# Attention's out products on the two row halves of TensorE, two token tiles together

## The chip, the cores and the metric

The kernel runs on one core of a Trainium2 chip. The metric is the device time of one execution in microseconds (us). Of the kernel before there are three runs, with a median of 717.38 us (716.96 to 717.64).

## What is computed

Eight sequences of 576 tokens pass through three stages. The change touches the first of them, a linear attention of 8 heads with 64 channels each:

```python
kv  = einsum('bhsd,bhse->bhde', k, v)        # one 64 x 64 matrix for a head
out = einsum('bhsd,bhde->bhse', q, kv)       # the out product
out = out / sqrt(mean(out**2, -1) + 1e-6) * g_norm
x   = out.transpose(0, 2, 1, 3).reshape(B, S, 512)
gate = sigmoid(causal conv of 5 taps over x, for each channel)
x = (gate * (x @ w_val)) @ w_out             # stage 2
h = gelu(x @ w_in); u, v = halves of h       # stage 3
x = x + (u * (w_sg @ layernorm(v) + b_sg)) @ w_out2
```

All of it is in float32. Stages 2 and 3 split each operand of a matmul into a high and a low part; the kv and out products are plain fp32 matmuls.

## The kernel before

Attention and stage 2 run together for a batch after the other, with several batches in flight; stage 3 follows for all batches. The tokens of a batch are four tiles of 128 and a fifth (number 4) that reaches back, TOK = [0, 128, 256, 384, 448], of which the last 64 columns are used. The 512 channels are four blocks j of 128, two heads each.

For a batch, `kv` (line 364) multiplies keys and values head by head into the two column halves of TensorE (line 379: 40 matmuls, with outputs on partitions 0 to 63 and 64 to 127). `kv_out` (line 384) copies the results into a block diagonal, `kvbd` (64 x 64 blocks, zeros beside them). `product` (line 395) makes the out product of one token tile: for each block j the q block (128 channels x 128 tokens) is the operand that is loaded, and `kvbd` (128 x 128) is the one that streams; the four results fill one PSUM bank of 512 words, all channels of 128 tokens. Then follow for the tile: `square` on ScalarE, `sums` on VectorE, `mean` and `root` on GpSimd, `scale` on VectorE (or ScalarE), `turn` (four transposes on TensorE into another bank), and from there `high` and `full` on ScalarE and `low` on VectorE, which write 4 channel blocks x 128 tokens of the operands of stage 2 and of the convolution (`taps`, `tap`). Channel block m of the convolution needs the tokens of all five tiles.

The order of all instructions is written out by hand in two strings, ORDER and STEADY, that a loop (line 950) walks through. In them o31 is batch 3's out product of tile 1; q, r, m, w, s, t are square, sums, mean, root, scale and turn; h, x and l are high, full and low; p is a tap, S a sigmoid; v and y are the two matmuls of stage 2 with z, Z, u and Y behind them; a, b and D are the splits of the weights (a1l is a matmul among them); kv3a and kv3b are the halves of kv. A number behind ~ puts that many small filler matmuls ahead of an operation (line 322). L stands for loads, all on SP's queue: LK1 loads k and v of batch 1, La1 a quarter of w_val (512 KB), LK0a and LV0a 512 KB of k and v, LM3 clears a part of V on GpSimd (`clear`, line 337). For batches 0 to 2 that clear was part of LK or LV (lines 356, 866, 875). Each engine works through its own instructions in this order. PSUM has eight banks, which `bank` (line 140) hands out in turn.

Of the kernel before, what the change touches and what calls it, by code (L numbers as in the profile page):

```python
# [44 lines left out]
r11 b0h p023 p001 o13 a2c r12 p002 m12 b11 p024 p030 m11* w11 o10 q14 q13 b12 b0l r13 q10 Lb3 r10 w12 Lb2 p031 v01 b0c
m13* S02 Lq2 p003 b13 p010 m10 w13 s11* w10 v03 s13* p032 s10* p011 t11 kv2 LK3 LM3 v00 p004 p012 p033 b1h v02 S00 k2a
p013 s12* b14 b20 p014 S01 b1s p034 z01 r14 z00 k2b h11 b2a S03 t13 Z01 b1+ Z00 g0L m14* t10 b21 t12 x13 x11 w14 b30
h10 s14 o22 o21~3 u00* l11 g0r z03 h13 Z03 z02 l10 l13 t14 h12 o24 l12 o23 b22 u01* o20 Lq3 LDa LDb q24 x10 q23 b3a
r23 Z02 q22 u03* x14 q20 q21 x12 b31 m23* w23 b23 b32 r22 b24 r21 r20 u02* m20* p110 b33 p120 r24 v11 p111 v12 p121
# [8 lines left out]
Z20 w31 p232 p233 s30 u20* o33 Dat LM4 s31 t30 q33 v22 Db0 h30 r33 q32 z21 m33* S22 w33 p234 Dba Y11 r32 g2X o34 Db1
S23 m32* s33 w32 Z21 t31 z22 v23 Y10 u21 g2r x31 g2L LDc Db2 q34 Lq4 Db3 Z22 x30 u22* kv4a/0-8 z23 Dbh h31 kv4a/8-12
s32 Z23 r34 kv4b Db4 m34* Dbs LDd t32 w34 u23 LK5 y20/0-11 h32 Dbt x32 Dca Dc1 Dc0 Dc2 t33 s34 y21/0-5 h33 l32 k4 l33  # L60
y20/11-1 y21/5-7 x33 Dc3 Dc4 Dch l31 LDe Dcs t34 y22 Dct x34 l30 p300 Dda p301 p310 p302 p320 o40 Y21 p303 y23 p330
p311 g3X Y20 Dd0 p312 q40 p304 o41 p321 S30 r40 v30 q41 p331 m40* w40 p322 Dd1 Dd2 p313 o42 r41 v31 q42 s40 m41* w41
Y22 z30 p323 p314 o43 p324 S31 Z30 t40 p332 v32 q43 r42 Y23 p333 S32 m42* u30* s41 r43 o44 z31 w42 z32 Z31 t41 Lq5 v33
p334 q44 m43* Z32 w43 Dd3 s42 Ddh S33 u31 g3r u32* s43 t42 r44 y30/0-9 Dds z33 m44* Dd4 Z33 LM5 Ddt LDf w44 h42 u33
t43 x42 y31/0-9 De0 Dea x40 s44 h41 g3L l42 x41 y30/9-2 x43 De1 y31/9-2 De2 y30/11-1 De3 y31/11-1 Deh t44 De4 y32 Des
LDg x44 Det p430 Df0 l41 p420 p410 y33 Dfa p411 p400 p431 Y32 Y31 p401 p412 v80 Y33 Df1 h40 Df2 p402 v81 p413 p421
kv5a/0-8 l40 kv5a/8-12 p403 kv5b p404 z80 v82 k5 z81 Y30 Df3 v83 Z81 z82 Z80 LK6 u81 Z82 u80* o50 z83 Dfh p414 o51 q50
Dfs h43 r50 y80/0-5 g4X u82* y81/0-5 l43 q51 y82/0-1 Z83 y80/5-1 r51 y81/5-1 y82/1-5 m50* Df4 w50 y83/0-4 Dft LDh
y80/6-2 p422 y81/6-2 Dga y82/6-2 y83/4-1 y80/8-1 Dg0 y81/8-1 m51* y82/8-1 u83 y83/5-2 w51 y80/9-2 y81/9-2 p432 y82/9-2
y83/7-4 Dg1 v40/0-3 Dg2 Dg3 Dgh y80/11-1 s50 y81/11-1 y82/11-1 y83/11-1 Dgs Y81 v40/3-9 S40 Dg4 s51 Y82 LDi Y83 p433  # L70
S41 o52 p423 t50 Dgt q52 t51 p424 Dha v41 Y80 p434 Dh0 Dh1 Dh2 Dh3 Dhh z40 Dhs o53 Z40 LM6 Dh4 v42 z41 LDj q53 r52 S43
Dht Z41 m52* g4L u40* Dia x51 h51 o54 Di1 w52 Di0 Di2 v43 r53 q54 Lq6 Dih Di3 S42 u41 Dis m53* Di4 w53 z42 LDk
kv6a/0-8 Dit Z42 kv6a/8-12 r54 Dja s52 h50 kv6b m54* u42* z43 x50 s53 t52 Z43 LK7 w54 Dj0 g4r Dj1 h52 Dj2 Dj3 Djh u43
y40 x52 LM7 Djs l50 s54 t53 Dj4 y41 x53 l52 LDl h53 Djt Dk0 Dka k6 Dk1 Dk2 Y40 Dk3 t54 l51 Dkh y42 x54 Dks l53 p500
Dk4 Dkt p520 LDm p501 p530 p502 o60 Dla Dl1 p531 y43 q60 p510 p532 p503 p521 o61 Dl0 r60 v50 p522 q61 m60* w60 g5X Dl2
p511 p504 p512 o62 p523 v51 q62 r61 S50 s60 m61* Y43 w61 p533 Y41 p524 o63 r62 t60 p513 q63 m62* v52 Dlh s61 S52 Dl3
Y42 p514 Dls z50 S51 r63 Z50 o64 Dl4 m63* w62 Dlt t61 Lq7 z51 v53 h61 LDn p534 Dma w63 q64 Dm0 g5L Z51 z52 x61 u51 S53
# [1041 lines left out]
```

## Time and profile before

| | |
|---|---|
| time, median of three runs | 717.38 us |
| the profiled execution, its own time | 717.08 us |
| its span, first to last instruction | 715.3 us |
| TensorE multiplies / weight loads | 706.0 / 618.3 us |
| VectorE | 571.8 us |
| ScalarE / GpSimd | 362.2 / 163.4 us |

Engines are named as in the profile: PE is TensorE's multiplies, PEld its weight loads, DVE VectorE, ACT ScalarE, POOL GpSimd, SP the queue that issues transfers. A row of a timeline has the start and the length of a group of instructions in us, engine, line, operation, tile written and tiles read, rows and columns of TensorE in use, the shape, and the number of instructions. An fp32 matmul shows as two loads and two multiplies. The end of a multiply is modelled in the profile and reaches past the start of the next one, so the pace of matmuls is read from starts.

### The profile page before, as it was taken

What the parts mean: (1) busy time and instruction counts of PE and PEld (TensorE: products, weight loads), DVE (VectorE), ACT (ScalarE), POOL (GpSimd) and SP (SyncE); (2) the same over time, 40 slices, a digit from 0 to 9 for tenths busy, and PEclk for the clock granted to TensorE, in tenths of its full rate; (3) what the DMA queues carried; (4) which work ended last, traced back from release to release, by engine and by line L of the source; (5) the groups of instructions that cost most, each with busy time, mean ns of one, the idle gap of its engine ahead of it and who ended that gap; (6) DMA issues with size and microseconds to landing.
All of it is one profiled execution on the core that took longest, in us unless ns stands there. A gap on an engine that the chain in (4) does not pass through costs nothing.

```text
span 715.3 us, 11743 instructions
## 1 busy us (share of the span) xinstructions
PE 706.0 (99%) x4462; PEld 618.3 (86%) x4462; DVE 571.8 (80%) x1111; ACT 362.2 (51%) x747; POOL 163.4 (23%) x180
## 2 busy tenths in 40 slices
PE   7999999999999999999999999999999999999998
PEld 7788888889888888899889888898899898898897
DVE  3999898989999999799867877767857767868662
ACT  2999947574657574664424434325434334335220
POOL 1558435444636443121000000100100100100000
PEclk9999999999999999999999999999999999999999
DMA  9994046336534105541231222123241122111302
GB/s 306 323 298 164 31 170 239 115 111 229 197 100 155 75 31 169 164 149 32 81 112 30 75 89 59 53 66 89 77 144 43 62 74 75 59 60 45 103 1 89
DMA packets 57241, 81.20 MB, mean 114 GB/s; under 512 B 3680, under 2 KB 30304, under 8 KB 56160
## 3 DMA queue, kind: packets, MB, share of 16 engines
q1 hardware_dynamic: 57184, 80.45, 33.7%
q8 instruction: 35, 0.57, 0.3%
q14 instruction: 22, 0.18, 0.1%
HBM read 61.56 MB, written 18.87 MB: 112 GB/s over the span
## 4 chain that ended last, share of the span: by engine, by line
PE 59%; DVE 2%; DMA 1%; issue 0%; ACT 0%; SPq 0%; DVEq 0%; ACTq 0%
PE sg L740 17%; PE out L303 14%; PE hv L631 13%; PE hu L303 12%; PE hur L303 2%; DVE G L499 1%; DMA raw<-y_main 1%; PE y L303 1%; PE val L303 0%; DVE T L531 0%; ACT X1h L608 0%; DVE cv L196 0%; DVE cv L191 0%; DVE cv L187 0%; DVE X1l L609 0%
## 5 line engine op out<-in xcount | busy, mean ns | idle before, releaser
L499 DVE SCALAR_TENSOR_TENSOR G<-X,cw,G 128x576 f32<-128x576 f32 x128 | 101.8, 827 | 4.2 <-ACT G L496 3.9
L643 POOL TENSOR_TENSOR bmv<-bmv,mhalf 128x1 f32<-128x1 f32 x36 | 21.5, 596 | 342.4 <-DVE bmv L642 342.4
L303 PE MATMUL y<-Z,WOh 128*128 128x512 f32 (+1 forms) x320 | 96.2, 375 | 0.0
L631 PE MATMUL hv<-wiv,X1h 128*128 128x512 f32 x256 | 83.3, 390 | 0.9 <-ACT X1h L608 0.9
L303 PE MATMUL out<-Z,K 128*128 128x512 f32 x256 | 83.0, 389 | 0.0
L303 PE MATMUL hu<-X1h,wiu 128*128 128x512 f32 x256 | 79.2, 391 | 0.0
L421 POOL TENSOR_TENSOR st<-st,mhalf 128x8 f32<-128x8 f32 x40 | 73.1, 1839 | 2.2
L303 PEld LDWEIGHTS y<-Z,WOh 128*128 128x128 f32 x320 | 57.9, 188 | 9.7
L620 ACT ACTIVATE T<-T 128x512 f32<-128x512 f32 x68 | 42.9, 631 | 42.3 <-DVE T L617 42.2
L303 PE MATMUL y<-Z,WOl 128*128 128x512 f32 (+1 forms) x160 | 58.0, 368 | 0.0
L631 PEld LDWEIGHTS hv<-wiv,X1h 128*128 128x128 f32 x256 | 47.7, 188 | 10.8 <-ACT X1h L608 1.4
L303 PEld LDWEIGHTS out<-Z,K 128*128 128x128 f32 x256 | 48.1, 188 | 9.9
L741 DVE SCALAR_TENSOR_TENSOR T<-sg,gln,WOl 128x288 f32<-128x288 f32 x64 | 32.8, 516 | 26.3 <-PE sg L740 26.2
L303 PEld LDWEIGHTS hu<-X1h,wiu 128*128 128x128 f32 x256 | 46.6, 188 | 8.3
L303 PE MATMUL hu<-X1l,wiu 128*128 128x512 f32 x128 | 50.0, 390 | 0.0
L631 PE MATMUL hv<-wiv,X1l 128*128 128x512 f32 x128 | 49.9, 390 | 0.0
L303 PE MATMUL out<-Z,V 128*128 128x512 f32 x128 | 49.8, 389 | 0.0
L752 ACT ACTIVATE Z<-T 128x512 fp32r<-128x512 f32 x32 | 20.1, 631 | 58.2 <-DVE T L751 58.2
L400 PEld LDWEIGHTS o<-kvbd,Q 128*128 128x128 f32 x320 | 39.9, 191 | 2.6 <-ACT kvbd L391 0.5
L400 PE MATMUL o<-kvbd,Q 128*128 128x128 f32 x320 | 40.7, 275 | 0.3 <-ACT kvbd L391 0.3
L303 PE MATMUL val<-X0h,WV 128*128 128x512 f32 x128 | 40.7, 399 | 0.0
L303 PE MATMUL val<-X1h,WV 128*128 128x512 f32 x128 | 40.0, 396 | 0.0
(183 smaller groups left out, 1708.6 us busy)
## 6 DMA issues: line engine op xcount, KB each, us to landing
y_main<-Y SPq DMA_DIRECT2D x8, 1024.0 KB, 4.7
raw<-y_main SPq DMA_DIRECT2D x32, 256.0 KB, 3.1
Y<-y_main SPq DMA_DIRECT2D x32, 256.0 KB, 3.9
out_dram<-Y SPq DMA_DIRECT2D x32, 256.0 KB, 2.3
Q<-in_qT_dram SPq DMA_DIRECT2D x7, 1152.0 KB, 6.3
K<-in_k_dram SPq DMA_DIRECT2D x7, 1024.0 KB, 7.3
V<-in_v_dram SPq DMA_DIRECT2D x7, 1024.0 KB, 9.1
raw<-in_w_in_dram SPq DMA_DIRECT2D x16, 256.0 KB, 4.8
```

The source lines that it names most:

```text
L303: nc.tensor.matmul(ps, lhsT=a[:, kt, msl], rhs=x[:, kt], start=(i == 0), stop=(i == 3 * NK - 1))
L400: nc.tensor.matmul(po[:, j * P:(j + 1) * P], lhsT=self.q[:, j, o:o + P], rhs=bd[:, j, :], start=True, stop=True)
L421: nc.gpsimd.tensor_tensor(st[:, 2], st[:, 1], mhalf, op=ALU.pow)
L499: stt(gate[:, m], x32[:, m, j:j + S], cw3[:, m, j:j + 1], gate[:, m], op0=ALU.mult, op1=ALU.add)
L620: act(w, w, AF.Tanh, scale=CG * AG)
L631: nc.tensor.matmul(ps, lhsT=a[:, kt], rhs=p2["wiv"][:, w, kt], start=(i == 0), stop=(i == 3 * NK - 1))
L643: nc.gpsimd.tensor_tensor(mv[:, 3:4], mv[:, 2:3], mhalf[:, 0:1], op=ALU.pow)
L740: nc.tensor.matmul(ps, lhsT=a[:, msl], rhs=w, start=(n == 0), stop=(n == len(mm) - 1))
L741: later(0, lambda: stt(vs[:, sl], ps, gln_s[:, m:m + 1], p2["bsg"][:, sl], op0=ALU.mult, op1=ALU.add))
L752: act(g[:, 0], x, AF.Copy)
```

## The change

The out products of two token tiles are made together. For tiles 0 and 1 (and 2 and 3) there are two banks; for each tile, block j and half a, one matmul loads the q of one head (64 partitions x 128 tokens), on the row half a of TensorE, and streams the head's 64 x 64 block of kv, 64 columns, into bank a. A bank then holds four heads of 256 tokens in place of eight heads of 128. The fifth tile is made as before, four matmuls of 128 columns, written in two strips. On the host the heads of q, k and v are put in the order 0, 4, 1, 5, 2, 6, 3, 7, so that block j holds heads j and j + 4, and bank a the heads of a consecutive half. `turn`, `high`, `full` and `low` keep their four transposes and their 512 elements for each bank, now two channel blocks x 256 tokens (`part`). In the order's text o00 and o02 are then the pairs of batch 0, while q, r, m, w, s, t, h, x and l with number 0 to 3 stand for a bank each. The two order strings become one, newly written: it holds the same operations but for o with tiles 1 and 3, which are gone, and LM0, LM1 and LM2, which are now named. At the start K0a and K0b are loaded ahead of the quarters 1 and 0 of w_val.

```diff
@@ -37,54 +37,50 @@
 ORDER = """
-W30 La0 La1 LK0a LV0a LK0b LV0b LK0c LV0c Lq0a Lq0b Lg La2 La3 Lb0 Lcw a1a a0a a01 a00 a10 kv0a a02 a11 a12 kv0b a13
-a14 a03 k03b k01b a0h k02b k03a k02a k00b k01a k00a a04 o01~3 q01 o03 r01 a20 q03 LK1 o02 a2a r03 a21 q02 o04 a3a m01*
...
-"""
-
-STEADY = """
...
+LK0a LK0b La1 LV0a La0 W30 LV0b LV0c LK0c LM0 Lq0a La2 Lq0b Lcw Lg La3 a1a Lb0 a11 a10 kv0a a00 a0a a01 a02 a12 kv0b
+a13 a03 k01b k03a LK1 k01a k02a k02b k00a a0h k00b a04 a1h k03b o00~3 a14 a20 a2a a1l q01 a21 q00 a22 r01 a2h o02 c0
+a23 m01* w01 q02 o04 q03 a30 r02 q04 Lq1 r00 m02* ca Lb2 w02 a24 b0a a2l Lb1 a3a r03 LDa s01* c1 b00 m03* a31 w03 a32
...
+Dc0 g2r Z21 t32 z20 v22 Dc1 Z20 Dc2 g2L S22 u20* Dch h33 h32 Dc3 y21/0-5 l30 Dcs x33 l31 x32 t34 Dc4 z22 o42 LDe l32
+Z22 o40 u21 x34 q42 u22* l33 o44 q43 r42 q41 y20/0-11 Dct q40 m42* u23 w42 p330 Dd0 r41 Y11 p320 p331 m41* LM5 y23 q44
...
 """
@@ -393,11 +389,24 @@
                             nc.vector.tensor_copy(bd[h, j, h], pk[h, :, h])
 
         def product(self, t):
-            o, bd = TOK[t], kvbd[self.b % 2]
-            self.tile[t] = {"po": own(bank("o"))}
-            po = self.tile[t]["po"]
-            for j in range(NK):
-                nc.tensor.matmul(po[:, j * P:(j + 1) * P], lhsT=self.q[:, j, o:o + P], rhs=bd[:, j, :], start=True, stop=True)
+            bd = kvbd[self.b % 2]
+            if t == 4:
+                po = own(bank("o"))
+                self.tile[t] = {"po": po}
+                po = po.rearrange("p (a j e) -> p j a e", a=2, j=NK)
+                for j in range(NK):
+                    nc.tensor.matmul(po[:, j], lhsT=self.q[:, j, TOK[4]:], rhs=bd[:, j].rearrange("p (a e) -> p a e", a=2),
+                                     start=True, stop=True)
+                return
+            po = [own(bank("o")) for a in range(2)]
+            for a in range(2):
+                self.tile[t + a] = {"po": po[a]}
+            for i in range(2):
+                o = TOK[t + i]
+                for j in range(NK):
+                    for a in range(2):
+                        h, c = slice(a * DH, (a + 1) * DH), (i * NK + j) * DH
+                        nc.tensor.matmul(po[a][:, c:c + DH], lhsT=self.q[h, j, o:o + P], rhs=bd[h, j, h], start=True, stop=True)
 
         def square(self, t):
             i = self.tile[t]
@@ -430,24 +439,31 @@
                i["st"][:, 2].unsqueeze(2).to_broadcast([P, 8, DH]), op=ALU.mult)
 
         def turn(self, t):
-            i, n = self.tile[t], P if t < 4 else REST
+            i = self.tile[t]
             pt = own(bank("xT"))
+            if t == 4:
+                i["pt"] = pt.rearrange("p (j e) -> p j e", j=NK)[:, :, P - REST:]
+            else:
+                i["pt"] = pt.rearrange("p (m e) -> p m e", m=2)
             for j in range(NK):
-                nc.tensor.transpose(pt[:, j * P:(j + 1) * P], i["xo"][:, j * P:(j + 1) * P], ident)
-            i["pt"] = pt.rearrange("p (j e) -> p j e", j=NK)[:, :, P - n:]
+                c = j if t == 4 else j % 2 * 2 + j // 2
+                nc.tensor.transpose(pt[:, c * P:(c + 1) * P], i["xo"][:, j * P:(j + 1) * P], ident)
+
+        def part(self, x, t, o=0):
+            c = t // 2 * 2 * P + o
+            return x[:, t % 2 * 2:t % 2 * 2 + 2, c:c + 2 * P]
 
         def at(self, t):
-            o, n = (TOK[t], P) if t < 4 else (MAIN, REST)
-            return x32[:, :, HALO + o:HALO + o + n]
+            return self.part(x32, t, HALO) if t < 4 else x32[:, :, HALO + MAIN:]
 
         def high(self, t):
-            act(self.xh[:, :, TOK[t]:TOK[t] + P], self.tile[t]["pt"], AF.Identity, scale=gcol_s)
+            act(self.part(self.xh, t), self.tile[t]["pt"], AF.Identity, scale=gcol_s)
 
         def full(self, t):
             act(self.at(t), self.tile[t]["pt"], AF.Identity, scale=gcol_s)
 
         def low(self, t, by=None):
-            xh, xl = (x[:, :, TOK[t]:TOK[t] + P] for x in (self.xh, self.xl))
+            xh, xl = (self.part(x, t) for x in (self.xh, self.xl))
             if by is None:
                 stt(xl, self.tile[t]["pt"], gcol_s, f32(xh), op0=ALU.mult, op1=ALU.subtract)
             else:
@@ -863,7 +879,7 @@
             piece[0]()
             piece[2]()
         elif what in ("K0c", "V0c"):
-            atts[0].load_kv((), (kind == "V",))
+            atts[0].load_kv((), (kind == "V",), clear=False)
         elif kind in "KV" and i[0] == "0":
             atts[0].load_kv(K0[i[1]], (kind == "V",), False)
         elif kind == "M":
@@ -872,7 +888,7 @@
             w_piece(i)[0]()
         elif kind in "KV":
             if kind == "K":
-                atts[int(i)].load_kv(clear=int(i) < 3)
+                atts[int(i)].load_kv(clear=False)
         elif kind == "q":
             atts[int(i[0])].load_q({"a": ((0, 2 * P),), "b": ((2 * P, S),), "": ((0, S),)}[i[1:]])
         elif what == "cw":
@@ -957,11 +973,6 @@
                 busy(int(op[1:]))
             elif op in ("kv0a", "kv0b"):
                 atts[0].kv("ab".index(op[3]), False)
-            else:
-                act_part(op.rstrip("*"), op[-1] == "*")
-        for op in STEADY.split():
-            if op[0] == "L":
-                load(op[1:])
             else:
                 act_part(op.rstrip("*"), op[-1] == "*")
     marks = [latest()] * 4
@@ -1086,10 +1097,12 @@
     import concourse.bacc as bacc
     from concourse.bass_utils import run_bass_kernel_spmd as run
 
+    turn = [i + j for j in range(4) for i in (0, 4)]
+    q, k, v = (np.asarray(x)[:, turn] for x in (q, k, v))
     host = {
-        "qT": np.asarray(q).transpose(0, 1, 3, 2).reshape(B, NK, P, S),
-        "k": np.asarray(k).transpose(0, 2, 1, 3).reshape(B, S, D),
-        "v": np.asarray(v).transpose(0, 2, 1, 3).reshape(B, S, D),
+        "qT": q.transpose(0, 1, 3, 2).reshape(B, NK, P, S),
+        "k": k.transpose(0, 2, 1, 3).reshape(B, S, D),
+        "v": v.transpose(0, 2, 1, 3).reshape(B, S, D),
         "gcol": np.concatenate([g_norm, g_norm]).reshape(P, 1),
         "w_val": moe_w_val,
         "conv_w": np.asarray(moe_conv_w).reshape(KC, NK, P).transpose(2, 1, 0).reshape(P, NK * KC),
```

## Rows read from the trace of the kernel before

**Rows 1.** page, busy us, share, instructions of an engine
```profile
PE 706.0 (99%) x4462; PEld 618.3 (86%) x4462; DVE 571.8 (80%) x1111; ACT 362.2 (51%) x747; POOL 163.4 (23%) x180
```

**Rows 2.** windows: start:end length, then PE, PEld, DVE, ACT, POOL busy, clock, DMA
```profile
0.00:30.00 30.00, 24.99 (x236) 21.00 (x238) 16.63 (x38) 15.68 (x37) 12.94 (x24) 1.00 0.99 326
30.00:210.00 180.00, 179.84 (x1399) 156.34 (x1399) 165.07 (x291) 129.46 (x299) 87.36 (x81) 1.00 0.51 172
210.00:270.00 60.00, 60.00 (x381) 50.74 (x380) 59.27 (x110) 41.21 (x79) 30.12 (x29) 1.00 0.22 79
```

**Rows 3.** waits of TensorE's loads, 0 to 300 us: us, times, longest
```profile
PEld xT L436 <- DVE T L429: 1.9, 4, 0.6
PEld xT L436 <- ACT T L427: 0.7, 3, 0.3
```

**Rows 4.** chain of waits up to 290 us: start, us, what
```profile
282.35 0.44 DVE cv L191
282.83 3.15 DMA raw<-y_main
```

**Rows 5.** timeline of multiplies around one out product: start, us, engine, line
```profile
95.50 0.39 PE L303 MATMUL y<-Z,WOh 128*128 128x512 f32 x1
95.73 1.05 PE L400 MATMUL o<-kvbd,Q 128*128 128x128 f32 x8
96.54 0.48 PE L303 MATMUL y<-Z,WOh 128*128 128x512 f32 x1
96.85 0.40 PE L303 MATMUL y<-Z,WOl 128*128 128x512 f32 x1
```

**Rows 6.** line 400, the out product: ns min/median/max, first and last start
```profile
L400 PEld LDWEIGHTS o<-kvbd,Q x320: 186/192/192, 16.2 to 248.1; 128*128 128x128 f32 x160
L400 PE MATMUL o<-kvbd,Q x320: 270/275/377, 16.2 to 248.2; 128*128 128x128 f32 x160
```

**Rows 7.** timeline of loads, then of multiplies, after a wait
```profile
292.27 0.19 PEld L631 LDWEIGHTS hv<-wiv,X1h 128*128 128x128 f32 x1 [1.35 <-ACT X1h L608]
292.38 0.42 PEld L303 LDWEIGHTS val<-XR,WV 128*128 128x128 f32 x2
292.27 0.50 PE L631 MATMUL hv<-wiv,X1h 128*128 128x512 f32 x1 [0.93 <-ACT X1h L608]
```

**Rows 8.** timeline of multiplies around one kv product
```profile
114.58 0.39 PE L303 MATMUL val<-X0l,WV 128*128 128x512 f32 x1
114.90 2.55 PE L379 MATMUL kv<-V,K 128*64 128x64 f32 x80
117.39 0.66 PE L436 MATMUL xT<-ident,T 128*128 128x128 f32 x4
```

**Rows 9.** loads of the first kv product, two cuts; then line 379
```profile
10.16 0.14 PEld L379 LDWEIGHTS kv<-V,K 128*64 128x64 f32 x2
10.16 0.20 PEld L379 LDWEIGHTS kv<-V,K 128*64 128x64 f32 x4
L379 PEld LDWEIGHTS kv<-V,K x640: 132/138/138, 10.2 to 222.5; 128*64 128x64 f32 x160
L379 PE MATMUL kv<-V,K x640: 222/222/271, 10.2 to 222.5; 128*64 128x64 f32 x160
```

**Rows 10.** behind a kv product: multiplies, next load; behind an out product: load
```profile
45.49 2.55 PE L379 MATMUL kv<-V,K 128*64 128x64 f32 x80
47.97 0.30 PEld L303 LDWEIGHTS val<-X0h,WV 128*128 128x128 f32 x2
96.51 0.19 PEld L303 LDWEIGHTS y<-Z,WOh 128*128 128x128 f32 x1
```

**Rows 11.** timeline of VectorE at the start
```profile
7.25 0.43 DVE L195 TENSOR_SCALAR wiv<-wiv 128x512 f32<-128x512 f32 x1 [7.25 <-ACT wiv L184]
11.12 0.42 DVE L196 TENSOR_SCALAR wiv<-wiv 128x512 int32<-128x512 int32 x1
15.13 0.65 DVE L393 COPY kvbd<-kv 64x64 f32<-64x64 f32 x4 [3.59 <-PE kv L379]
```

More of the change, by code (lines that the diff above doesn't have):

```diff
@@ L39 @@
 ORDER = """
-W30 La0 La1 LK0a LV0a LK0b LV0b LK0c LV0c Lq0a Lq0b Lg La2 La3 Lb0 Lcw a1a a0a a01 a00 a10 kv0a a02 a11 a12 kv0b a13
-a14 a03 k03b k01b a0h k02b k03a k02a k00b k01a k00a a04 o01~3 q01 o03 r01 a20 q03 LK1 o02 a2a r03 a21 q02 o04 a3a m01*
-w01 a30 m03* r02 o00 q04 a31 a0l a22 a32 a23 m02* q00 w02 a1h Lq1 a1l s01* a0c w03 a33 r00 ca s02 r04 b0a a2h s03 a24
-b01 t01 a3h t02 m00* m04 c0 Lb1 h02 w00 w04 t03~1 c1 a2l s00 h03 h01 a34 x01 b00 t00 c2 s04 x02 kv1 x03 x00 b02 h00
-l03 c3 a1c b03 c4 b04 c5 k1b k1a t04 x04 a3l l02 p020 LK2 b1a o11 l01 l00 q11 o12 a3c o14 p021 p000 b10 g0X p022 q12
@@ L45 @@
[L45 to L49, printed above, removed]
@@ L58 @@
[L58 to L62, printed above, removed]
@@ L63 @@
[L63 to L77, printed above, removed]
@@ new lines @@
+a13 a03 k01b k03a LK1 k01a k02a k02b k00a a0h k00b a04 a1h k03b o00~3 a14 a20 a2a a1l q01 a21 q00 a22 r01 a2h o02 c0
+a23 m01* w01 q02 o04 q03 a30 r02 q04 Lq1 r00 m02* ca Lb2 w02 a24 b0a a2l Lb1 a3a r03 LDa s01* c1 b00 m03* a31 w03 a32
+r04 a1c t01 a3h s02 m00* a0l w00 x01 c2 s03 h01 c3 t03~1 c4 m04 a33 a0c LM1 b01 t02 w04 s00 x03 h02 a34 t00 a2c b02
+h03 l02 kv1 h00 s04 x00 l00 x02 c5 b03 b04 t04 k1b LK2 k1a a3l l01 x04 l03 p020 o10 p000 p021 o12 q10 p001 q11 o14 r10
+q12 q13 p022 v02 b1a Lq2 r13 b0h Lb3 b10 m13* m10 LDb p023 a3c w13 p030 r12 p010 r11 v00 w10 m12 b11 b2a p011 s13*
@@ new lines @@
+p002 m11* w12 b12 b0l q14 p012 s10* v01 p024 w11 p013 s12* p003 LM2 b13 p031 t13 S02 kv2 p004 s11* z02 p032 Z02 p014
+b0c t10 S00 p033 t12 k2a v03 b14 h13 r14 S01 h12 p034 m14* w14 k2b l12 x10 o24 z01 x12 z00 u02* g0X t11 h10 l13 o22
+x13 s14 LM3 b1h o20~3 l10 S03 b1s h11 b21 Z00 Lq3 b1+ q20 LK3 u00* l11 v13 q23 x11 z03 Z01 g0L b30 Z03 t14 u01* r23
+g0r r20 q24 q22 u03* y00 r24 x14 r22 b3a m20* b20 q21 m22* b31 m23* v11 b32 w22 Y00 Daa r21 p120 b22 m24 m21* p130
+p121 w21 b3h b33 v12 p131 s22* w20 p122 b34 b2h Da1 p100 b3s w23 y01 b23 s21* p132 w24 b3+ s20* b2s p123 y03 b24 s24*
@@ new lines @@
+p133 p101 Y01 t21 b2+ p110 t20 p124 y02 s23* p111 p134 Y03 p112 x21 h21 p102 t23 S13 kv3a/0-8 p113 h23 kv3a/8-12 p114
+S12 kv3b Y02 l23 h20 p103 v10 k3 Da0 Da2 p104 S11 Dah z11 g1X S10 Da3 z12 Z11 o34 g1L x23 u11* z10 Z12 t24 o32 x24 Da4
+x20 u12* l21 o30 Z10 z13 q32 u10 Lq4 t22 Z13 l20 LDd q33 u13* y13 LK4 q31 r33 g1r r31 q30 m33* Das h22 r30 p230 LM4
+y10 Dat w33 l22 q34 x22 p231 Dba r34 m31* g2X w31 p200 Db0 Db1 v23 r32 p210 Db2 Y10 s33 m30* m32* p220 m34* Db3 p232
+w32 Y13 Dbh s31 t33 p201 y12 w30 p211 p202 w34 s30 p233 t31 y11 s32 Dbs s34 p221 Db4 p203 LDc t30 p234 kv4a/0-8
@@ new lines @@
+kv4a/8-12 p204 S23 Dbt kv4b S20 z23 Dca p212 h31 v21 LK5 k4 p213 Z23 p222 Y12 p214 p223 S21 v20 h30 p224 x30 z21 x31
+Dc0 g2r Z21 t32 z20 v22 Dc1 Z20 Dc2 g2L S22 u20* Dch h33 h32 Dc3 y21/0-5 l30 Dcs x33 l31 x32 t34 Dc4 z22 o42 LDe l32
+Z22 o40 u21 x34 q42 u22* l33 o44 q43 r42 q41 y20/0-11 Dct q40 m42* u23 w42 p330 Dd0 r41 Y11 p320 p331 m41* LM5 y23 q44
+s42 w41 Dda r40 p310 p332 r43 Dd1 y22 m43* Dd2 w43 s41 p311 p321 Y23 Ddh Dd3 p300 y21/5-7 p333 Dds s43 p301 y20/11-1
+Y21 t42 Dd4 t41 r44 v32 p322 m44* w44 p334 p312 m40* s44 v30 w40 p313 p323 Ddt p314 Dea v31 g3X p324 Y22 h41 p302 S32
@@ new lines @@
+s40 h42 p303 Y20 t40 S33 De1 t44 De0 p304 v33 LDf g3L S30 z32 x44 De2 S31 De3 z30 Deh x40 t43 De4 Des z33 LDg kv5a/0-8
+h43 z31 Lq5 kv5a/8-12 Z30 Det Z31 u30* kv5b h40 Z32 l40 x43 v82 u32* Dfa x42 u31 v83 x41 Df0 g3r l41 p400 y31/0-9 Df1
+z82 p420 Df2 l43 p430 p401 p410 v81 Z33 p402 k5 Df3 Df4 y31/9-2 Dfh z83 LDi v80 z81 Dfs l42 LK6 p431 y30/0-9 p411 p403
+z80 o50 p412 u33 o52 q50 p432 y30/9-2 r50 y31/11-1 y30/11-1 p433 Y31 y33 p421 Dft p413 Dga Dg0 p422 y32 Y33 Dg1 q51
+Dg2 Y30 r51 q52 p404 m51* w51 p414 v40/0-3 S40 Z83 o54 Dg3 Y32 u83 m50* Z81 p434 w50 v40/3-9 Z80 q54 Dg4 Z82 LDh r54
@@ new lines @@
+Dgh u82* r52 y82/0-1 Lq6 v43 u80* z40 s51 Dgs q53 S43 m54* r53 LM6 w54 Dgt s50 Dha y81/0-5 S41 u81 y80/0-5 Dh0 p423
+m53* y82/1-5 w53 z43 y80/5-1 y83/0-4 Dh1 y80/6-2 p424 y81/5-1 y82/6-2 y83/4-1 y80/8-1 y82/8-1 Dh2 y81/6-2 g4r y83/5-2
+Dh3 Dhh y82/9-2 Dh4 y81/8-1 y80/9-2 Dhs s54 y81/9-2 LDj y83/7-4 m52* y80/11-1 Dht y82/11-1 w52 y83/11-1 y81/11-1 Di0
+Y82 t50 g4X t51 Y81 g4L Dia v41 Z40 Di1 Di2 Z43 u40* s52 S42 s53 h50 u43 x50 t54 Di3 Dih z41 t53 Dis v42 Z41 Di4 h51
+Dit LDk h53 u41 Dja Dj0 x54 Dj1 Dj2 x51 kv6a/0-8 Dj3 x53 z42 kv6a/8-12 Djh Dj4 Y80 l51 kv6b Djs LDl Z42 l50 Y83 u42*
@@ new lines @@
+t52 k6 LK7 y40 Djt LM7 x52 l53 p510 Dk0 Dka p511 p520 Dk1 o62 p521 Dk2 o60 q63 Dk3 p512 Y40 o64 q60 p522 p500 Dk4 y43
+p523 q62 LDm g5X r63 q61 p524 h52 Dkh l52 p530 Dks y41 r60 S52 m63* Dkt w63 q64 p501 Dla Dl0 Dl1 r62 m60* y42 w60 Dl2
+r64 Dlh Y41 p502 m62* p513 w62 r61 v52 p503 Dl3 s60 Dls s63 m61* m64* Dl4 t60 w61 z52 LDp v50 h60 s62 Lq7 Z52 p504 w64
+Y42 p514 p531 t63 t62 Dlt h63 p532 v51 Dma S51 p533 S50 Dm0 s64 Y43 h62 g5L Dm1 v53 z50 x60 Dm2 Z50 p534 x62 u50* z51
+g5r l62 Z51 t64 u52* s61 kv7a/0-8 x64 l60 Dmh kv7a/8-12 p610 Dm3 u51 kv7b p600 Dms l63 S53 Dm4 x63 p601 t61 LDn
@@ new lines @@
+y51/0-4 z53 x61 k7 p611 y50/0-9 Dmt Z53 p612 Dna u53 h61 o74 Dn0 p620 Dn1 l61 y50/9-2 p602 y51/4-2 o70 Dn2 p613 o72
+q71 Dn3 Dn4 q74 p603 LDo y51/6-6 q72 p621 Dnh q73 Dns r72 y50/11-1 Y51 y52 r74 m72* q70 Dnt Y50 r73 r71 r70 m71* v60
+w72 p622 Y52 p630 Do0 p604 Doa m74* p631 m70* S60 w74 s72 y53 Do1 p623 w71 Do2 z60 Do3 p632 w70 v61 s71 p614 p633 S61
+Doh Do4 t72 g6X s70 Dos LDq v62 h72 z61 m73* w73 p624 Z61 Z60 p634 S62 Dot u60* t71 S63 s74 v63 z62 h71 Y53 u61 Z62
+g6L Dp0 g6r s73 u62* Dpa x72 t74 z63 t70 Dp1 y61/0-8 Z63 Dp2 x74 Dp3 u63 Dph x70 Dp4 Dps l71 t73 LDr p700 y60/0-8 Dpt
@@ L88 @@
+x71 p701 Dqa Dq0 x73 Dq1 y61/8-1 Dq2 h70 y60/8-1 y61/9-2 Dq3 p702 Dqh y60/9-2 p710 y63 Dqs l70 Dq4 p703 LDs Dqt p704
+Dra p720 y61/11-1 Dr0 y60/11-1 Dr1 y62 Y61 Dr2 p721 Drh p730 Dr3 p722 Drs l72 Dr4 Drt p731 Dsa h73 Ds0 Ds1 Y62 p732
+Y60 Ds2 Y63 p723 Dsh S70 Ds3 p711 LDt Dss l73 p712 p733 p713 p734 p724 S73 p714 S72 Ds4 S71 Dst
 """
```

15 lines of the change are left out of this document (removed).

## Prediction

> **What bounds the kernel now.** I read the shares of the span first: TensorE multiplies 706.0 of 715.3 us and VectorE works 571.8 [rows 1]. A share over the whole span could hide a stage with another limit, so I cut the attention stage, where the change lies, into stretches [rows 2]: from 30 to 210 us TensorE is busy for 179.84 of 180.00 and VectorE for 165.07; from 210 to 270 us TensorE for 60.00 of 60.00 and VectorE for 59.27, all at a granted clock of 1.00, the 2.4 GHz level. So TensorE is the limit throughout, and VectorE stands right behind it late in the stage. The waits of TensorE's loads up to 300 us are small [rows 3]: 1.9 and 0.7 us on the scaled products, all near the start. The chain that ends the stage runs over VectorE, whose last cast at 282.35 frees the buffer of the load at 282.83 [rows 4]. What the change is worth is therefore first TensorE's own time for the out products, and then what VectorE lets through.
>
> **What an out product costs now.** Behind a wide matmul (y) the next one starts after 0.23 us (95.50 to 95.73). One tile's product starts at 95.73 in the place of a y, that y starts at 96.54 and the next at 96.85 [rows 5]. Without the product the second y would have come at 95.73 + 0.23 = 95.96, so the product costs 0.89 us. The trace shows 320 multiplies and 320 weight loads for 40 products [rows 6], so each of a product's four fp32 matmuls is two loads with two multiplies: eight steps of 0.111 us. The change touches the four full tiles of eight batches, 32 products in 16 pairs: 1.78 us a pair now, 28.5 us in all.
>
> **Which half of a step sets its length** decides the case, because load and multiply lie beside each other. The load is the q block, 128 columns wide; the multiply streams 128 columns. The change halves only the second: a multiply streams 64 columns, and 16 matmuls a pair take the place of 8, so 32 loads of 128 columns in the place of 16, each 64 rows high. The load alone is seen where TensorE had waited [rows 7]: one load begins at 292.27 and the next at 292.38, 0.11 us later, while the multiply of the first is a 512-wide one of 0.50 us that sets no such pace. So a 128-wide load holds the load path for 0.11 us, the whole step of today. Streaming half as many columns shortens nothing that ends last.
>
> **Whether the halves load side by side.** The kv product shows two halves at work, those of the columns: 80 steps lie between its start at 114.90 and the next transpose at 117.39, 0.031 us each [rows 8]. Its first two loads of at least 0.132 us each both fit in 0.14 us, its first four in 0.20 [rows 9]: the two halves load at once, and each half steps every 0.06 us with 64-wide loads. Loads of 64 columns last 0.138 us and those of 128 columns 0.192 [rows 6, 9], so the time goes with the columns. I carry that to the row halves: two streams side by side, each with 16 loads of 128 columns at 0.111 us = 1.78 us a pair, which is today's price, a gain of nothing. No row shows a load of 64 rows. The bounds: if a load of half the rows takes half the time, a half steps every 0.058 us as in kv, a pair costs 16 x 0.058 = 0.93 us and the pairs give back 16 x 0.85 = 13.6 us; if the halves take turns, 32 x 0.111 = 3.56 us, a loss of 16 x 1.78 = 28.5 us. I take zero, since width and side-by-side loading both have a row and a price by height has none.
>
> The Trainium skill (TensorE: Matmul & The Clock Gate, section LDWEIGHTS (loading the stationary operand)) says that a load takes its time by columns, and that a load of 32 rows by 128 columns is as long as one of 128 by 128. By it the lower bound falls away; no row here can show it.
>
> **What is added: changes of shape.** The kv product needs halves too, and its borders show a price. It starts 0.32 us after the val before it (114.58 to 114.90), against 0.23 for an out product behind y: 0.09 [rows 5, 8]. Another kv product's last multiply, 0.22 us long [rows 9], begins at 45.49 + 2.55 - 0.22 = 47.82, and the next load only at 47.97: 0.15 us. Behind an out product the load follows at once (its last multiply at 95.73 + 1.05 - 0.28 = 96.50, the load at 96.51) [rows 5, 6, 10]. And the first multiply waits for its own load instead of finding it done, 0.11 less what the entry already holds, say 0.06. That is 0.30 us a visit, 0.2 to 0.4. In the new order the two pairs of a batch stand next to each other for TensorE in six batches; in batch 0 a split matmul (a1l) lies between, in batch 2 the three fillers of o20~3: 10 visits, 3.0 us. None of it is hidden, as TensorE has no idle time there.
> The Trainium skill (TensorEngine Tiling (Array Packing), section Tiling Modes) says that a change of mode drains the engine; the 0.15 us behind kv agrees.
>
> **Edits with one answer.** The fifth tile still runs four 128-wide products, written in two strips: nothing. Squares, sums, scales, transposes, high, low and full parts keep their count and their 512 elements; only the view is 2 x 256 for 4 x 128. The heads' new places cost the host's copy alone. Both lists hold the same operations but for the pairs and the three clears named by themselves.
>
> **The new order.** Pairing makes the first square of a pair wait for both tiles, up to 0.89 us more, in front of scale and transpose; other matmuls stand between, and where they don't (the start), TensorE waits 2.6 us today [rows 3], so the bound is 2 us lost or 2.6 us won. The loads of a1 and a0 move behind K0a, K0b (and V0a for a0): two and three pieces of 512 KB more ahead of them, at 326 GB/s [rows 2] 3.2 and 4.8 us. VectorE's work on them begins at 7.25 and ends at 11.54, then it idles 3.59 us until 15.13 [rows 11]; so most of the delay disappears there and 0 to 1 us stays. V0a is the fourth piece in both lists, V0b the sixth, so kv0 starts when it did. The clears of V go to POOL later, and so its queue is freer; nothing waited on that for long. I book 0 for the order, -1.5 to +1.5.
>
> **The sum.** The profiled execution took 717.08 us (715.3 of span), 0.3 under the median of 717.38. 717.38 + 0 + 3.0 + 0 = 720.4 us, its own range 717.5 to 723.
>
> **The rivals.**
> 1. *Half loads are faster* (the other side). Then -13.6 + 3.0 = -10.6, 706.8 us, if VectorE follows. It idles 14.93 us between 30 and 210 and 0.73 between 210 and 270 [rows 2], and its chain ends the stage [rows 4]; no row says how much of that idle time lies where it can be used. If only half of the gain gets through, it is 712; I say 708. It decides from a load step under about 0.10 us. For it: kv halves at 0.06 us. Against: those loads are half as wide.
> The Trainium skill (TensorEngine Tiling (Array Packing), section Overview) promises up to twice the speed where the contracted dimension is 64 or less, which is the case here; that would be this rival.
> 2. *The halves take turns at loading.* +28.5 + 3.0: 749 us. For it: two loads on all rows are 0.11 us apart [rows 7]. Against: kv's two loads at once [rows 9].
> 3. *Inside a half, load and multiply don't overlap*: 16 x (0.111 + 0.055) = 2.66 us a pair, +14.1 + 3.0: 734.5 us. Against: a kv half steps at 0.06 us with both in it.
> 4. *The order pays for the borders*: the 2.6 us of early waits go and the borders cost 2: 716 to 717, or less.
>
> **Chances.** Forecast 0.46, of which 0.10 is within 0.2%; rival 1 0.29; rival 2 0.12; rival 3 0.07; rival 4 0.06, two thirds of it faster. A difference under 0.2% (1.4 us) is about what this measurement can't tell from none. Faster 0.29 + 0.04 = 0.33; same 0.10 + 0.02 = 0.12; slower 0.36 + 0.12 + 0.07 = 0.55. The range must leave out no more than 0.2: from rival 1's full gain to rival 3, 706 to 735, leaving out rival 2 and the ends.
>
> **What the changed profile would show.** Right: 32 multiplies a pair over 1.8 us, a load of o about every 0.055 us over both halves (0.111 in one), gaps of 0.15 us behind each visit, TensorE still full from 30 to 270 us. Wrong downward: a pair in 0.95 us and the stage's end ahead of 282 us. Wrong upward: loads of o 0.11 us apart, a pair in 3.5 us.

## The result and the profile after

The changed kernel takes 722.74 us (median of 4 runs, 722.19 to 722.90), the kernel before, run beside it, 717.20 (716.96 to 717.64): 1.0075 times as long, with a 95% interval of 1.0063 to 1.0088. That is 5.5 us slower, on the forecast's side (720.4) and 2.3 us above it. The profiled execution has a span of 721.1 us against 715.3.

The page of the changed kernel, busy us and instructions of an engine, answers to [rows 1]:

```profile
PE 710.9 (99%) x4718; PEld 620.8 (86%) x4718; DVE 571.7 (79%) x1111; ACT 360.8 (50%) x747; POOL 163.0 (23%) x180
```

The windows of the changed kernel, with the columns of [rows 2] (PE, PEld, DVE, ACT, POOL, clock, DMA share, GB/s):

```profile
30.00:210.00 180.00, 177.62 (x1592) 152.94 (x1592) 163.91 (x285) 130.26 (x302) 87.71 (x83) 1.00 0.50 172
210.00:270.00 60.00, 60.00 (x405) 50.58 (x404) 58.13 (x112) 38.03 (x75) 32.62 (x30) 1.00 0.24 84
```

There are 256 more loads and multiplies, the clock is the same, and VectorE has the same work. TensorE is busy longer in total, but between 30 and 210 us it now stands still for 2.38 us, where it stood still for 0.16 before [rows 2]. So two things are to be found: time that counts as busy, and time that doesn't.

Where it was lost is seen at one place that both kernels reach after the last out product: the first multiply of `hur`. The fences are the timelines of the kernel before, of the one after, and of two experiments below, e1 (the old out products in the new order) and e8 (the same, but both banks of a pair ready only at its end):

```profile
311.30 0.40 PE L303 MATMUL hur<-XR,wiu 128*128 128x256 f32 x2
```
```profile
317.10 0.40 PE L299 MATMUL hur<-XR,wiu 128*128 128x256 f32 x2
```
```profile
312.22 0.40 PE L299 MATMUL hur<-XR,wiu 128*128 128x256 f32 x2
314.26 0.40 PE L299 MATMUL hur<-XR,wiu 128*128 128x256 f32 x2
```

The changed kernel is 5.8 us late there, and its span is 5.8 us longer: everything is lost up to here and, on balance, nothing after. e1 is 0.9 us late (its repetition e9 too, 312.21), e8 3.0.

The out product itself: the source row (duration ns min/median/max, first and last start) of the changed kernel, which answers to [rows 6].

```profile
L409 PEld LDWEIGHTS o<-kvbd,Q x512: 183/189/189, 15.0 to 238.7; 64*128 64x128 f32 x171
L409 PE MATMUL o<-kvbd,Q x512: 271/272/321, 15.0 to 238.7; 64*128 64x64 f32 x171
```

A load of 64 rows lasts 189 ns where one of 128 rows lasted 192. Two pairs that stand next to each other, on the timeline of multiplies of the changed kernel:

```profile
165.58 0.39 PE L299 MATMUL y<-Z,WOh 128*128 128x512 f32 x1
165.90 3.79 PE L409 MATMUL o<-kvbd,Q 64*128 64x64 f32 x64
169.62 0.50 PE L299 MATMUL y<-Z,WOh 128*128 128x512 f32 x1
169.96 0.39 PE L299 MATMUL y<-Z,WOl 128*128 128x512 f32 x1
```

and on the timeline of its loads, in three cuts that end inside the visit or behind it:

```profile
165.90 0.19 PEld L409 LDWEIGHTS o<-kvbd,Q 64*128 64x128 f32 x2 [0.35 <-issue]
165.90 0.30 PEld L409 LDWEIGHTS o<-kvbd,Q 64*128 64x128 f32 x4 [0.35 <-issue]
165.90 3.65 PEld L409 LDWEIGHTS o<-kvbd,Q 64*128 64x128 f32 x64 [0.35 <-issue]
```

The first two loads lie together inside 0.19 us, so they run at once; the first four inside 0.30, so the second couple begins 0.11 us after the first. Sixty-four loads begin within 3.65 - 0.19 = 3.46 us: 0.112 us for each couple, the step of a 128-wide product before the change. The halves work side by side and gain nothing, and the visit (a stretch of half-row products between other work of TensorE) has an entry (0.32 us from y to o, 0.23 before [rows 5]) and an exit.

### The profile page after: what moved, and what is told of

Its sections match the earlier page's. It is cut to its first block, busy times and chain, and to the rows that moved or that the text cites. A ratio compares the mean times of both kernels' runs of the same rounds, so it can differ in the third digit from the quotient of the medians.

```text
span 721.1 us, 12263 instructions
## 1 busy us (share of the span) xinstructions
PE 710.9 (99%) x4718; PEld 620.8 (86%) x4718; DVE 571.7 (79%) x1111; ACT 360.8 (50%) x747; POOL 163.0 (23%) x180
## 4 chain that ended last, share of the span: by engine, by line
PE 60%; DVE 3%; issue 0%; DVEq 0%
PE sg L756 16%; PE out L299 14%; PE hv L647 14%; PE hu L299 12%; PE y L299 2%; PE hur L299 2%; DVE G L515 1%; PE val L299 1%; DVE T L547 0%; DVE Z L556 0%; DVE X1l L468 0%; DVE cv L183 0%; DVE cv L187 0%; DVE cv L191 0%; DVE cv L190 0%
## 5 line engine op out<-in xcount | busy, mean ns | idle before, releaser
L659 POOL TENSOR_TENSOR bmv<-bmv,mhalf 128x1 f32<-128x1 f32 x36 | 19.6, 544 | 336.2 <-DVE bmv L658 336.2
L556 POOL TENSOR_TENSOR Z<-T,Z 128x512 fp32r<-128x512 f32 (+1 forms) x23 | 29.5, 1292 | 52.7 <-ACT Z L552 52.7
L632 ACT ACTIVATE T<-hv 128x512 f32<-128x512 f32 x36 | 21.3, 591 | 27.7 <-PE hv L647 27.1
```

The costliest lines, as they stand in the source:

```text
L556: (nc.gpsimd.tensor_tensor if on_pool else tt)(zl, self.t[m], f32(zh), op=ALU.subtract)
L632: act(w, ps, AF.Square)
L659: nc.gpsimd.tensor_tensor(mv[:, 3:4], mv[:, 2:3], mhalf[:, 0:1], op=ALU.pow)
```

## The experiments

Each kernel is the changed kernel with one more edit. Times of the kernel before, run beside them: 717.22 us for e1 to e7, 717.45 for e8 and e9.

**e1: the new order without the halves.**

```diff
-                    for a in range(2):
-                        h, c = slice(a * DH, (a + 1) * DH), (i * NK + j) * DH
-                        nc.tensor.matmul(po[a][:, c:c + DH], lhsT=self.q[h, j, o:o + P], rhs=bd[h, j, h], start=True, stop=True)
+                    nc.tensor.matmul(po[i][:, j * P:(j + 1) * P], lhsT=self.q[:, j, o:o + P], rhs=bd[:, j], start=True, stop=True)
```

> The changed kernel with the two tiles of a pair multiplied as before, four matmuls of 128 columns on all rows for each tile, one tile in each bank; all else, the order above all, stays. Channels and tokens come out in other places than downstream reads them. Theory 1 (load-bound halves cost the same, 3.0 us go to the ten changes of shape, the rest of the 5.5 us to the order): 722.7 - 3.0 = 719.7 us. Rival a (the order does it all): 722.7, no change against the changed kernel. Rival b (the changes of shape do it all): 717.2, as before.

Measured: 718.02 us, ratio 1.0012 (0.9999 to 1.0025). The new order with the old products is 0.8 us behind the kernel before, and the remaining 4.7 us came with the edit that e1 undoes. The same place as above, two tiles' products of e1 on its timeline of multiplies:

```profile
161.80 0.39 PE L299 MATMUL y<-Z,WOh 128*128 128x512 f32 x1
162.03 3.73 PE L407 MATMUL o<-kvbd,Q 128*128 128x128 f32 x32
165.83 0.40 PE L299 MATMUL y<-Z,WOl 128*128 128x512 f32 x1
```

From the y in front to the second y behind: 165.83 - 161.80 = 4.03 us, in the changed kernel 169.96 - 165.58 = 4.38. The visit with halves costs 0.35 us more, and as its steps keep their 0.11 us, the price lies at its two ends. Ten visits at that price would make 3.5 us. That leaves over a microsecond of the 4.7 to something else, which e8 takes up.

**e2: all 128 rows loaded, 64 columns streamed.**

```diff
-                        nc.tensor.matmul(po[a][:, c:c + DH], lhsT=self.q[h, j, o:o + P], rhs=bd[h, j, h], start=True, stop=True)
+                        nc.tensor.matmul(po[a][:, c:c + DH], lhsT=self.q[:, j, o:o + P], rhs=bd[:, j, h], start=True, stop=True)
```

> The changed kernel with the same 16 matmuls of 64 streamed columns a pair, each on all 128 rows (the other head's block is zero), so nothing can lie side by side. Theory 1 (a 128-wide load holds its rows for 0.111 us, and the two halves load at once): 32 steps of 0.111 = 3.56 us a pair in place of 1.78, +28.5 us, less 3.0 for changes of shape that are gone: 748 us. Rival (the step of 0.056 us seen in the changed kernel is the price of a 64-column multiply, and nothing runs side by side): 16 pairs as now, less the borders: 720 us.

Measured: 747.31 us, ratio 1.0415 (1.0387 to 1.0443). Timeline of multiplies of e2:

```profile
180.32 7.25 PE L409 MATMUL o<-kvbd,Q 128*128 128x64 f32 x64
187.38 0.47 PE L299 MATMUL y<-Z,WOh 128*128 128x512 f32 x1
```

The 64 steps take 187.38 - 180.32 = 7.06 us, 0.110 us each, with 64 columns streamed as with 128. So it is the load that sets the step, and what keeps the halves from costing 28 us is that two of them load at once.

**e3: loads half as wide.** Each matmul of a half is cut into two of 64 tokens, so that a load is 64 rows by 64 columns.

```diff
-                    for a in range(2):
-                        h, c = slice(a * DH, (a + 1) * DH), (i * NK + j) * DH
-                        nc.tensor.matmul(po[a][:, c:c + DH], lhsT=self.q[h, j, o:o + P], rhs=bd[h, j, h], start=True, stop=True)
+                    for n in range(2):
+                        for a in range(2):
+                            h, c = slice(a * DH, (a + 1) * DH), (i * NK + j) * DH
+                            nc.tensor.matmul(po[a][n * DH:(n + 1) * DH, c:c + DH], lhsT=self.q[h, j, o + n * DH:o + (n + 1) * DH],
+                                             rhs=bd[h, j, h], start=True, stop=True)
```

> The changed kernel with each matmul of a pair cut into two of 64 tokens: 64 x 64 quarters of TensorE, 32 matmuls a pair, loads of 64 columns. Theory 1 (the width of the load is the limit, parts load side by side): 16 steps a quarter at 0.058 = 0.93 us a pair, -13.6 us: 709 us. Rival a (a limit of about 0.029 us for each multiply issued, which is also what kv shows with two halves): 64 x 0.029 = 1.86 us a pair, +1.3: 724 us. Rival b (the quarters take turns in twos): as now, 723 us.

Measured: 713.6 us, ratio 0.9951 (0.9931 to 0.9971): faster than both kernels. Timeline of multiplies of e3, two pairs next to each other:

```profile
226.84 2.10 PE L410 MATMUL o<-kvbd,Q 64*64 64x64 f32 x128
228.86 0.50 PE L299 MATMUL y<-Z,WOh 128*128 128x512 f32 x1
```

Its 128 steps take 228.86 - 226.84 = 2.02 us with the exit, where the halves took 169.62 - 165.90 = 3.72. Of the 13.7 us that the expectation took off the changed kernel, 9.1 came. The ten visits together, from their first multiply to the next work of TensorE, take 19.05 us where the changed kernel's take 30.55, so 11.5 us came in the visits and some of it is lost again between them. Inside the visits there are new stops, the longest of them here:

```profile
35.23 1.37 PE L410 MATMUL o<-kvbd,Q 64*64 64x64 f32 x74
37.14 1.04 PE L410 MATMUL o<-kvbd,Q 64*64 64x64 f32 x54 [0.54 <-issue]
```

In the midst of a product TensorE stops for 0.54 us, and nothing that the profile shows holds it back. Why is open. The list of waits of the loads (us, times, longest), 0 to 300 us, has such waits in e3 and also in the changed kernel, where they stand at the beginnings of products:

```profile
PEld o L410 <- issue: 3.7, 7, 1.6
PEld o L409 <- issue: 2.6, 6, 1.2
```

So 1.1 us of them are new in e3.

**e4: the loads at the start in their old places**, the rest of the list as in the changed kernel.

```diff
-LK0a LK0b La1 LV0a La0 W30 LV0b LV0c LK0c LM0 Lq0a La2 Lq0b Lcw Lg La3 a1a Lb0 a11 ...
+W30 La0 La1 LK0a LV0a LK0b LV0b LK0c LV0c LM0 Lq0a Lq0b Lg La2 La3 Lb0 Lcw a1a a11 ...
```

> The changed kernel with the first loads in the order of the kernel before (a0 and a1 ahead of k and v). Theory 1, order part: the wait for a1 and a0 at the start costs 1 to 2 us of the changed kernel, so 721 to 722 us. Rival (the start's loads are hidden, the waits of the order come from the pairs): 722.7, no change.

Measured: 725.28 us, ratio 1.0115 (1.0086 to 1.0143): 2.5 us slower than the changed kernel, where 1 us faster or nothing had been expected. The waits of TensorE's multiplies up to 60 us (us, times, longest), e4 and then the changed kernel:

```profile
PE l L270 <- DVE WV L187: 1.7, 1, 1.7
```
```profile
PE l L270 <- DVE WV L187: 0.4, 1, 0.4
```

TensorE waits 1.3 us longer for VectorE's work on WV. The first kv product waits 0.9 us for its V pieces in e4 and not in the changed kernel, but that is not the loads' doing: e5, with the new places, waits as long (the lines stand below, with the prediction), and e4's second pair starts no later than the changed kernel's (19.54 us against 19.82). Behind the wait for WV e4 has something that the changed kernel has not, a lower clock. A window of e4 (PE, PEld, DVE, ACT, POOL, clock, DMA share, GB/s); the changed kernel has a clock of 1.00 there:

```profile
20.00:30.00 10.00, 7.34 (x51) 4.92 (x49) 7.96 (x18) 8.45 (x22) 7.29 (x8) 0.84 1.06 353
```

The clock is at 0.50 (1.2 GHz) from 27 to 33 us. At hur this execution is 1.7 us behind the changed kernel (318.81 against 317.10); the six executions of e4 take 723.42 us (mean clock 0.999) to 728.12 (0.987). About 1.0 us of the 1.7 stands already behind the wait for WV (25.40 us against 24.39 for the multiply that waits), and the other 0.7 came in the stretch of the lower clock. What the old places would cost at the full clock no run shows.

**e5: one half's multiplies all ahead of the other's.**

```diff
-            for i in range(2):
-                o = TOK[t + i]
-                for j in range(NK):
-                    for a in range(2):
+            for a in range(2):
+                for i in range(2):
+                    o = TOK[t + i]
+                    for j in range(NK):
```

> The changed kernel with the 16 matmuls of a pair in another order: all eight of row half 0, then all eight of row half 1, in place of taking turns. The work is the same. Theory 1 (halves load at once, but only where the next matmuls in the queue go to the other half): 32 steps of 0.111 = 3.56 us a pair, +28.5: 751 us. Rival (TensorE looks far enough ahead to find the other half's work): 722.7, no change.

Measured: 767.6 us, ratio 1.0702 (1.0679 to 1.0725); expected were 751. Loads of one visit of e5, in three cuts: inside the first run of one half, behind the change of half, and inside the second run:

```profile
106.25 1.41 PEld L409 LDWEIGHTS o<-kvbd,Q 64*128 64x128 f32 x12 [0.17 <-issue]
106.25 1.91 PEld L409 LDWEIGHTS o<-kvbd,Q 64*128 64x128 f32 x20 [0.17 <-issue]
106.25 2.81 PEld L409 LDWEIGHTS o<-kvbd,Q 64*128 64x128 f32 x28 [0.17 <-issue]
```

Inside a run of one half the loads follow one another by 0.11 us (11 steps in 1.41 - 0.19 = 1.22 us), with nothing beside them. The next eight begin within 0.50 us, 0.06 each: around the change of half the last four of one half and the first four of the other go side by side. Behind them the step is 0.11 again. TensorE takes a step of the other half no more than those four early here, so the written order of the multiplies has to alternate.

By that the expectation's 28.5 us were too many. At the full clock a visit of two pairs takes 52 steps in place of 32, one of a single pair 28 in place of 16; for six and four visits that is 168 x 0.112 = 18.8 us, an estimate. Measured are 44.9 us over the changed kernel. The other 26 go with the clock, whose mean over the 763.9 us of the profiled execution was 0.959; no run separates them. The fall, in windows of all of e5's work (PE, PEld, DVE, ACT, POOL, clock, DMA share, GB/s):

```profile
108.00:110.00 2.00, 2.00 (x27) 2.00 (x24) 1.61 (x3) 1.50 (x4) 0.75 (x2) 1.00 0.00 0
110.00:112.00 2.00, 2.00 (x19) 2.00 (x18) 0.69 (x1) 0.28 (x1) 1.51 (x3) 0.67 0.00 0
112.00:114.00 2.00, 2.00 (x10) 1.88 (x11) 0.00 (x0) 0.00 (x0) 2.00 (x3) 0.50 0.01 4
118.00:120.00 2.00, 2.00 (x11) 1.61 (x10) 2.00 (x6) 1.79 (x4) 0.41 (x2) 1.00 1.02 394
```

**e6: six more visits.** One filler stands between the two pairs in the six batches where they were joined; six lines change like this one:

```diff
-... p000 p021 o12 q10 p001 ...
+... p000 p021 o12~1 q10 p001 ...
```

> The changed kernel with one filler matmul (128 columns on all rows) ahead of the second pair in the six batches where the two pairs stand next to each other, so 16 visits to the halves in place of 10. The fillers themselves cost 6 x 0.22 = 1.3 us. Theory 1 (a visit costs 0.35 us as the trace of the changed kernel shows at its borders): 6 x (0.22 + 0.35) = 3.4 us more: 726.1 us. Rival (borders are free and the loss comes from waits in the order): 724.0 us.

Measured: 725.97 us, ratio 1.0118 (1.0103 to 1.0132): 3.2 us over the changed kernel. Less the 1.3 us of the fillers, that is 1.93 us for six visits, 0.32 us each. Timeline of multiplies of e6, a pair cut off by its filler:

```profile
237.67 2.00 PE L409 MATMUL o<-kvbd,Q 64*128 64x64 f32 x32
239.61 0.49 PE L320 MATMUL o<-ident 128*128 128x128 f32 x2
240.02 2.00 PE L409 MATMUL o<-kvbd,Q 64*128 64x64 f32 x32
241.96 0.50 PE L299 MATMUL y<-Z,WOh 128*128 128x512 f32 x1
```

From the first multiply to the y behind it is 4.29 us, in the changed kernel 3.72; less 0.22 for the filler, the added visit costs 0.35 us here.

**e7: the quarters with the second q load earlier**, against the waits of e3.

```diff
-... Lq0a La2 Lq0b Lcw Lg ...
+... Lq0a Lq0b La2 Lcw Lg ...
```

> The quarters kernel with the second part of batch 0's q loaded ahead of w_val's quarter 2 (a2). TensorE waited 1.24 us for it at 19.8 us in the quarters kernel. If that wait ended last: 713.6 - 1.2 = 712.4 us. Rival (the later a2 costs as much, as the loads' order did in the run with the loads as before): 713.6 to 715 us.

Measured: 714.24 us, ratio 0.9974 (0.9957 to 0.9992). Nothing is gained over e3. The waits of TensorE's multiplies up to 60 us, e3 and then e7:

```profile
PE o L410 <- DMA Q<-in_qT_dram: 1.2, 1, 1.2
PE l L270 <- DVE WV L187: 0.4, 1, 0.4
```
```profile
PE l L270 <- DVE WV L187: 1.5, 1, 1.5
PE o L410 <- issue: 1.3, 1, 1.3
```

The wait for q is gone, and others stand in its place: 1.1 us more for WV, as the rival had it, and 1.3 us in the midst of the second pair. The granted clock was 0.57 on the mean from 26 to 30 us too, where e3 kept 1.00. So e7 doesn't show what the wait for q alone is worth.

**e8 and e9: when the banks are ready.** The changed kernel's halves fill both banks up to the last multiply of the pair. e8 does that with the old products, in turns between the two tiles; e9 is e1 once more beside it, one tile's bank filled first.

```diff
-            for i in range(2):
-                o = TOK[t + i]
-                for j in range(NK):
-                    for a in range(2):
...
+            for j in range(NK):
+                for i in range(2):
+                    o = TOK[t + i]
+                    nc.tensor.matmul(po[i][:, j * P:(j + 1) * P], lhsT=self.q[:, j, o:o + P], rhs=bd[:, j], start=True, stop=True)
```

> The run with the wide products in the new order (718.0 us) with one thing more: the eight matmuls of a pair take turns between the two tiles, so that both banks are ready at the end of the pair, as in the changed kernel, and not the first one at its middle. Work and shapes are the same; channels and tokens again come out in other places. Theory 1 (of the 4.7 us between the wide products and the changed kernel 3.4 are borders, and 1.3 are waits because both banks come at the end): 719.3 us. Rival (the 1.3 us have another cause): 718.0 us, no change.

> The run with the wide products in the new order once more, beside the one with turns on the same chip: 718.0 us.

Measured: e8 720.02 us, ratio 1.0035 (1.0022 to 1.0049); e9 718.15, ratio 1.0010 (1.0002 to 1.0018). The two differ in nothing but the order of the multiplies inside a pair, and by 1.9 us. The windows of e8 and then of e9, 30 to 210 us (PE, PEld, DVE, ACT, POOL, clock, DMA share, GB/s):

```profile
30.00:210.00 180.00, 177.72 (x1409) 154.37 (x1410) 167.05 (x291) 131.04 (x304) 89.07 (x85) 1.00 0.51 172
```
```profile
30.00:210.00 180.00, 179.44 (x1419) 155.83 (x1418) 168.79 (x294) 131.09 (x303) 90.63 (x84) 1.00 0.50 172
```

TensorE stands still for 2.28 us in e8 and for 0.56 in e9; in the changed kernel it was 2.38. One chain behind it is the same in e8 and in the changed kernel. ScalarE's timeline of the changed kernel, first square of a pair and later the scales:

```profile
63.82 1.09 ACT L415 ACTIVATE T<-o 128x512 f32<-128x512 f32 x2 [1.45 <-PE o L409]
80.17 1.74 ACT L436 ACTIVATE T<-o,st 128x64 f32<-128x64 f32 x8 [1.14 <-POOL st L430]
```

and TensorE's timeline of the changed kernel, of e8, and of e9 at the transposes that follow:

```profile
80.67 0.60 PE L450 MATMUL xT<-ident,T 128*128 128x128 f32 x4
81.97 0.66 PE L450 MATMUL xT<-ident,T 128*128 128x128 f32 x4 [0.70 <-ACT T L436]
```
```profile
79.32 0.60 PE L448 MATMUL xT<-ident,T 128*128 128x128 f32 x4
80.62 0.66 PE L448 MATMUL xT<-ident,T 128*128 128x128 f32 x4 [0.70 <-ACT T L434]
```
```profile
78.03 1.20 PE L448 MATMUL xT<-ident,T 128*128 128x128 f32 x8
```

Where a bank comes ready at the pair's middle, its squares, roots and scales start earlier and eight transposes run through; where both come at its end, ScalarE idles first (1.45 us), then GpSimd's roots and the scales are late, and TensorE stands 0.70 us between the transposes. This chain holds 0.7 of the 2.05 us by which e8 is behind e9 at hur. About 1.0 us stands already ahead of the second batch's products, which begin at 35.62 us in e8 and at 34.59 in e9: 0.3 at the second pair, which waits for the load of q, and the rest at transposes of the first batch that wait for a tile scaled on VectorE. TensorE in e9 and then in e8:

```profile
27.64 1.09 PE L448 MATMUL xT<-ident,T 128*128 128x128 f32 x8
28.68 1.09 PE L448 MATMUL xT<-ident,T 128*128 128x128 f32 x8 [0.64 <-DVE T L436]
```

Behind the fourth batch's products (91.33 and 89.28 us) nothing more is lost.

## Why the prediction was right, and where it was off

**The balance.** From the kernel before over e9 and e8 to the changed kernel one thing is added at a time, so the steps between their ratios make up the whole: the order 0.0010 (0.7 us), both banks ready only at the pair's end 0.0025 (1.8 us), the halves 0.0040 (2.9 us); together 0.0075. The intervals of the ratios leave each step about 1 us of play. The starts of hur in the profiled executions give the same split: 0.9, 2.05 and 317.10 - 314.26 = 2.84 us. For the halves that is 0.28 us for each of ten visits; e6 gives 0.32, the single places above 0.35. So the halves cost 2.8 to 3.5 us, at the borders, since the steps between keep their pace.

**The load sets the step: right.** Two pairs of halves begin 64 loads in 3.46 us; e2 halves the streaming and keeps 0.110 us a step. The price by height that no row of before had is 189 ns for 64 rows against 192 for 128. The Trainium skill (TensorE: Matmul & The Clock Gate, section LDWEIGHTS (loading the stationary operand)) says that columns and not rows make a load's time; the trace agrees.

**Halves side by side: right**, with the first two loads inside 0.19 us. Rival 2 (turns) would have been 749 us, and e2, whose loads do take turns, is 747.31. Rival 3 falls with the 0.112 us of a couple. Rival 1 falls with it too, as it wanted a step under about 0.10 us: half the rows (189 ns) shorten no load. What shortens one is half the width, as e3 shows. The Trainium skill (TensorEngine Tiling (Array Packing), section Overview) has up to twice the speed where the contraction, or the free dimension of an operand, is at most 64. With the contraction and the streamed columns at 64 no pair got faster; with the loaded columns at 64 as well, a visit of two pairs went from 3.72 to 2.02 us, 1.84 times as fast.

**Borders: right in size.** Forecast were 0.30 us a visit and 3.0 in all, from the edges of the kv product [rows 8, 10]; measured 0.28 to 0.35 a visit and 2.8 to 3.5 in all. The entry is the 0.09 us that kv had. The 0.06 in the sum for the first load was an assumption, and no run separates it from the exit.

**The order: the mis-sized term.** "I book 0 for the order, -1.5 to +1.5" was 2.5 us short (0.7 + 1.8). The prediction saw that the first square of a pair waits for both tiles and then said that "other matmuls stand between". They do, but not in all places: TensorE's idle time between 30 and 210 us rose from 0.16 to 2.38 us. For the start, where it saw that nothing stands between, it set a possible gain of 2.6 us against the loss; about 1.0 us of the 1.8 was lost just there. The wait was to be costed as a chain over the engines that read the banks, not as TensorE's own delay of 0.89 us. The 2.5 us lie outside the term's own range; put in afterwards they make the sum 722.9, and 722.74 was measured, 0.3 us inside the upper end of the forecast's own range (723).

**"So kv0 starts when it did"** stands, though the changed kernel's trace seems to speak against it. The multiplies of the changed kernel, and then of e5, which has the same loads in the same order:

```profile
11.69 2.55 PE L375 MATMUL kv<-V,K 128*64 128x64 f32 x80
```
```profile
10.18 1.15 PE L375 MATMUL kv<-V,K 128*64 128x64 f32 x32
12.23 1.92 PE L375 MATMUL kv<-V,K 128*64 128x64 f32 x48 [0.90 <-DMA V<-in_v_dram]
```

In the kernel before kv started at 10.16 [rows 9]. It starts when the 60 multiplies of the filler W30 are through, and these took 8.38 us before, 8.40 in e5 and 9.92 in the changed kernel. A late start saves the wait for V: kv ends at 14.24 and at 14.15. Of the loads of a1 and a0, booked at 0 to 1 us of loss, e4 shows no loss: with the old places every execution was slower. Rival 4 (the order pays for the borders) falls with e1 and e9: the order as a whole gains nothing, it costs 0.7 to 0.8 us (e9's interval is 0.1 to 1.3).
